# Output tiles by token parity, a last tile in two column halves and a shorter list of end waits, in a recurrent-attention and MLP kernel

## The chip, the cores and the metric

The kernel runs on one core of one Trainium2 chip. The metric is the device time of one execution in microseconds (us), smaller is better. A profiled execution also gives a span, from the first to the last instruction; it is about 1.7 us shorter than the device time of the same execution (182.9 against 184.67 us for the kernel before).

A result names a state for each run: slow when it is over 1.5% above the fastest run *of the same kernel in the same comparison*.

Names used below: TensorE is PE in the profile (its weight loads PEld), VectorE is DVE, ScalarE is ACT, GpSimd is POOL, SyncE is SP. Psum is the memory that the matmuls write here, a semaphore a counter that instructions wait for, and the granted clock the share of TensorE's full clock that the profile records.

## The reference

A gated recurrent attention feeds a two-layer MLP with a squared relu.

```python
# q, k, v, alpha: (4 batches, 8 heads, 768 tokens, 48), float32
state = zeros(B, H, D, D)
for t in range(S):
    state = alpha[:, :, t, :, None] * state + einsum('bhd,bhe->bhde', k[:, :, t], v[:, :, t])
    y[:, :, t] = einsum('bhd,bhde->bhe', q[:, :, t], state)
x = y.transpose(0, 2, 1, 3).reshape(3072, 384)
h = x @ w_in                       # 384 -> 2048
out = maximum(h, 0) ** 2 @ w_out   # 2048 -> 384, float32
```

## The kernel before

The work is cut into 12 units g of 256 tokens. A unit is loaded (alpha, k, q, v), its attention is computed in pairs of tokens, its output x is transposed into `XT`, and then the MLP runs: first layer (`s1`, weights w_in), relu, square, second layer (`s2`, weights w_out), store. A small list scheduler in the kernel orders every engine's instructions once, before the run, with modelled times; on the chip ACT, to take the engine that matters below, worked through its list in that order (in before_again it stood 8.07 us at one instruction, with the next in its list behind it).

A chunk of x holds 128 tokens in the partition order (parity j, pair t). The kernel before keeps that order through the first layer and lets the relu put the tokens back in sequence, by writing with a step of two elements:

```python
# s1: 6 matmuls of 256 columns into one 512-column psum half
rin  = psH[hb].rearrange("p (x j t) -> p x j t", j=2, t=64)
rout = RR[rb][:].rearrange("p (x t j) -> p x j t", j=2, t=64)      # step of 2 elements
add("act", lambda e: e.activation(rout, rin, AF.Relu), ..., alts={"dve": ...max(rin, 0)...})
# square into GT; s2: 16 matmuls of 384 columns per output tile of 128 consecutive tokens
r0 = b * S + i * T + 128 * jq
add("sp", lambda e: e.dma_start(out[r0:r0 + 128, :], OSB[ob][:]), ...)
```

The end waits for the semaphore of every DMA of the program:

```python
final = [(self.dma_sems[k], 16 * n) for k, n in self.dma_count.items()]    # 30 semaphores
...
if e == "sp":
    for s, v in final:
        eng.wait_ge(s, v)
```

The loads are gated on each other's landing (a number is a unit, `"a"` its alpha); the inputs go out from SP, the weights from GpSimd:

```python
AFTER = {("win", 0): (1, "a"), ("win", 1): (1, "a"), 2: ("win", 0), ("wout", 0): (2, "a"),
         ("wout", 1): (2, "a"), 3: ("wout", 0)}
```

Each unit's v is cast to bf16 on whichever of GpSimd and ACT the scheduler finds free first. For the third unit (g = 2) it chose ACT, in front of that unit's logarithm:

```python
add("pool", lambda e: e.tensor_copy(vout, vin), 830, p0 + 900, reads=[("raw", r, 3)], ...,
    name=f"vc{g}", alts={"act": (lambda e: e.activation(vout, vin, AF.Copy), act_ns(2 * HD))})
```

```text
ACT's list around it (from the built program):  ... relu, square,
  Activation vbf<-raw 128x768   waits for v of unit 2        <- the cast
  Activation lab<-prd           the ln of unit 2, needed by TensorE's next matmuls
```

## Time and profile before

| | us |
|---|---|
| timed runs | 194.54, 193.52, 195.4 (median 194.54) |
| the profiled run | 184.67 (span 182.9, granted clock 1.00) |

The page of the profile, engines (busy time, share of the span, instructions), and its chain of work that ended last, followed back from the last instruction, at each step to what released it:

```profile
PE 176.7 (97%) x2325; PEld 138.6 (76%) x2325; DVE 128.2 (70%) x220; ACT 127.6 (70%) x217; POOL 19.3 (11%) x27
...
PE 80%; DMA 15%; SPq 2%; issue 1%; ACT 0%
PE psO L828 34%; PE psWH L797 31%; DMA raw<-in_alpha_dram 6%; DMA win<-in_moe_w_in_dram 5%; DMA wout<-in_moe_w_out_dram 5%; PE psX L666 3%; PE psX L659 2%; PE psZ L639 2%; PE psX L720 2%; PE psX L759 2%; SPq L491 2%; PE psWH L537 2%; PE psX
```

TensorE is busy 97% of the span and holds 80% of the chain. Groups of instructions: line, engine, operation, output from input, count | busy us, mean ns | idle time before:

```profile
L807 ACT ACTIVATE rr<-psWH 128x512 bf16<-128x512 f32 x78 | 56.0, 754 | 16.4 <-PE psWH L797 16.4
...
L809 DVE TENSOR_SCALAR rr<-psWH 128x512 bf16<-128x512 f32 x18 | 13.2, 739 | 2.7 <-PE psWH L797 2.5
...
L747 ACT ACTIVATE xbf<-psX 128x768 bf16<-128x768 f32 x12 | 9.7, 810 | 9.4 <-PE psZ L639 7.0 <-PE psX L666 2.2
...
L551 ACT ACTIVATE eq<-psWH 128x384 f32<-128x384 f32 x10 | 4.9, 490 | 0.3
```

L807 is the relu with the step of two. L747 and L551 are other ACT instructions that read psum, 768 and 384 columns, without it, in 810 and 490 ns; between them 512 columns would take about 600 ns by my estimate, not 754.

The chain in order of time (start, us, what), until TensorE takes over:

```profile
4.30 4.88 DMA raw<-in_alpha_dram
9.47 8.55 DMA win<-in_moe_w_in_dram
18.04 5.69 DMA raw<-in_alpha_dram
24.02 8.38 DMA wout<-in_moe_w_out_dram
32.45 1.48 PE psO L828 x8
```

So there are three parts. The start is bound by loads: alpha of the second unit, w_in, alpha of the third, w_out. The middle starts with the first w_out matmul at 32.45 us and is bound by TensorE. The end begins at 174.6 us, with the last first-layer matmul. The table by stretches (length, then the busy us of PE, PEld, DVE, ACT and POOL, clock, DMA share, GB/s) cut at those two points:

```profile
0.00:32.40 32.40, 29.81 (x412) 23.90 (x412) 24.42 (x56) 22.04 (x35) 5.66 (x14) 1.00 1.01 232
32.40:174.60 142.20, 142.01 (x1884) 111.96 (x1885) 102.88 (x163) 103.47 (x179) 13.62 (x14) 1.00 0.73 168
174.60:182.90 8.30, 4.85 (x31) 2.77 (x29) 0.85 (x2) 2.06 (x4) 0.00 (x0) 1.00 0.13 47
```

TensorE is busy 142.01 of the 142.20 us in the middle. Nothing here explains why the timed runs are 10 us longer than the profiled one.

### The profile page before, as it was taken

What the parts mean: (1) busy time and instruction counts of PE and PEld (TensorE: products, weight loads), DVE (VectorE), ACT (ScalarE), POOL (GpSimd) and SP (SyncE); (2) the same over time, 40 slices, a digit from 0 to 9 for tenths busy, and PEclk for the clock granted to TensorE, in tenths of its full rate; (3) what the DMA queues carried; (4) which work ended last, traced back from release to release, by engine and by line L of the source; (5) the groups of instructions that cost most, each with busy time, mean ns of one, the idle gap of its engine ahead of it and who ended that gap; (6) DMA issues with size and microseconds to landing.
All of it is one profiled execution on the core that took longest, in us unless ns stands there. A gap on an engine that the chain in (4) does not pass through costs nothing.

```text
span 182.9 us, 5327 instructions
## 1 busy us (share of the span) xinstructions
PE 176.7 (97%) x2325; PEld 138.6 (76%) x2325; DVE 128.2 (70%) x220; ACT 127.6 (70%) x217; POOL 19.3 (11%) x27
## 2 busy tenths in 40 slices
PE   7998999999999999999999999999999999999992
PEld 5786886766788688787878787788787787788760
DVE  6399678797979988968978939769749736433220
ACT  4662899476878778679769868678667746677541
POOL 3030021123023011202103210000000000000000
PEclk9999999999999999999999999999999999999999
DMA  5999999999999999999999990713613410110202
GB/s 148 322 279 200 249 239 192 230 253 277 214 277 225 313 219 292 233 325 234 325 279 227 295 212 6 156 49 59 104 45 61 104 43 0 47 43 7 83 0 86
DMA packets 73495, 31.80 MB, mean 174 GB/s; under 512 B 69376, under 2 KB 72448, under 8 KB 73472
## 3 DMA queue, kind: packets, MB, share of 16 engines
q1 hardware_dynamic: 72384, 28.32, 65.3%
q0 software_dynamic: 1088, 3.15, 9.4%
q8 instruction: 18, 0.29, 0.6%
q14 instruction: 5, 0.04, 0.1%
HBM read 25.17 MB, written 4.72 MB: 163 GB/s over the span
## 4 chain that ended last, share of the span: by engine, by line
PE 80%; DMA 15%; SPq 2%; issue 1%; ACT 0%
PE psO L828 34%; PE psWH L797 31%; DMA raw<-in_alpha_dram 6%; DMA win<-in_moe_w_in_dram 5%; DMA wout<-in_moe_w_out_dram 5%; PE psX L666 3%; PE psX L659 2%; PE psZ L639 2%; PE psX L720 2%; PE psX L759 2%; SPq L491 2%; PE psWH L537 2%; PE psX L828 1%; PE psZ L720 1%; PE psZ L603 0%
## 5 line engine op out<-in xcount | busy, mean ns | idle before, releaser
L797 PE MATMUL psWH<-xt,win 128*128 128x256 bf16 x576 | 73.8, 275 | 0.6 <-DMA win<-in_moe_w_in_dram 0.5
L828 PE MATMUL psO<-wout,gt 128*128 128x384 bf16 x368 | 70.6, 327 | 0.6 <-DMA wout<-in_moe_w_out_dram 0.6
L797 PEld LDWEIGHTS psWH<-xt,win 128*128 128x128 bf16 x576 | 65.0, 145 | 5.7 <-DVE xt L765 0.9
L807 ACT ACTIVATE rr<-psWH 128x512 bf16<-128x512 f32 x78 | 56.0, 754 | 16.4 <-PE psWH L797 16.4
L828 PEld LDWEIGHTS psO<-wout,gt 128*128 128x128 bf16 x368 | 34.4, 98 | 19.2 <-DMA wout<-in_moe_w_out_dram 0.9
L813 DVE TENSOR_TENSOR gt<-rr 128x512 bf16<-128x512 bf16 x54 | 23.0, 431 | 21.8 <-ACT rr L807 21.5
L816 ACT ACTIVATE gt<-rr 128x512 bf16<-128x512 bf16 x41 | 25.2, 626 | 2.1 <-DVE rr L809 1.5
L835 ACT ACTIVATE osb<-psO 128x384 f32<-128x384 f32 x21 | 10.3, 491 | 12.7 <-PE psO L828 12.7
L747 ACT ACTIVATE xbf<-psX 128x768 bf16<-128x768 f32 x12 | 9.7, 810 | 9.4 <-PE psZ L639 7.0
L809 DVE TENSOR_SCALAR rr<-psWH 128x512 bf16<-128x512 f32 x18 | 13.2, 739 | 2.7 <-PE psWH L797 2.5
L729 DVE TENSOR_TENSOR pm<-psX,caus 128x1024 bf16<-128x1024 f32 x12 | 14.7, 1222 | 0.6 <-PE psZ L720 0.4
L729 DVE TENSOR_TENSOR pm<-psZ,caus 128x1024 bf16<-128x1024 f32 x12 | 14.6, 1217 | 0.1
L589 DVE TENSOR_TENSOR qks<-raw,ek 128x768 bf16<-128x768 f32 x12 | 11.7, 971 | 3.4 <-ACT ek L516 3.2
L878 PE MATMUL psO<-zero 128*128 128x256 bf16 x81 | 12.5, 309 | 1.3 <-DVE zero L412 1.3
L589 DVE TENSOR_TENSOR qks<-raw,eq 128x768 bf16<-128x768 f32 x12 | 11.4, 952 | 0.4 <-POOL eq L564 0.2
L692 DVE TENSOR_TENSOR tmp<-psZ,sbd 128x384 f32<-128x384 f32 x8 | 4.4, 555 | 9.2 <-PE psZ L639 9.2
L878 PEld LDWEIGHTS psO<-zero 128*128 128x128 bf16 x81 | 8.4, 110 | 3.0 <-DVE zero L412 1.2
L765 DVE COPY xt<-psX 128x768 bf16<-128x768 bf16 x10 | 5.6, 556 | 5.8 <-PE psX L759 5.8
L585 POOL CAST vbf<-raw 128x768 bf16<-128x768 f32 x6 | 5.7, 956 | 33.1 <-DMA raw<-in_v_dram 21.6
L666 PE MATMUL psX<-vbf,pm 64*128 64x48 bf16 x384 | 6.9, 181 | 0.0
L531 ACT ACTIVATE lab<-prd 128x384 bf16<-128x384 f32 x10 | 5.2, 516 | 1.9 <-DVE prd L528 1.5
L666 PEld LDWEIGHTS psX<-vbf,pm 64*128 64x128 bf16 x384 | 5.6, 93 | 0.8
(104 smaller groups left out, 159.4 us busy)
## 6 DMA issues: line engine op xcount, KB each, us to landing
raw<-in_alpha_dram SPq DMA_DIRECT2D x12, 384.0 KB, 4.5
raw<-in_k_dram SPq DMA_DIRECT2D x12, 384.0 KB, 4.8
raw<-in_q_dram SPq DMA_DIRECT2D x12, 384.0 KB, 5.2
raw<-in_v_dram SPq DMA_DIRECT2D x12, 384.0 KB, 5.2
out_dram<-osb SPq DMA_DIRECT2D x24, 192.0 KB, 2.6
win<-in_moe_w_in_dram POOLq DMA_DIRECT2D x2, 768.0 KB, 9.9
wout<-in_moe_w_out_dram POOLq DMA_DIRECT2D x2, 768.0 KB, 10.1
kqt<-qks SPq DMA_TRANSPOSE x18, 4.8
```

The lines of the kernel that those rows point to most:

```text
L589: add("dve", lambda e, a=a, E=E: e.tensor_tensor(QKS[qs][:, a, :, :, 0:D], RAW[r][:, 1 + a].rearrange("p h j d -> p j h d"), E[la][:].rear ...
L666: ins = pe.matmul(psX[:, c, h * D:(h + 1) * D], PM[pm][64 * c:64 * c + 64, n // 2, rr_, n % 2, jk, :], VBF[vb][64 * c:64 * c + 64, h, jk, ...
L729: add("dve", lambda e, hf=hf, psT=psT: e.tensor_tensor(PM[pm][:, hf].rearrange("p r n j t -> p (r n) (j t)"), psT[:, :, :].rearrange("p r ...
L747: add("act", lambda e: e.activation(XBF[x2][:], psX[:, :, 0:HD], AF.Copy), act_ns(2 * HD), p0 + 6100, reads=[("ps", "X", 0), ("ps", "X", 1 ...
L797: ins = pe.matmul(psH[hb][:, i * n:(i + 1) * n], WIN[:, kk, hidden(fj)], mov, start=(kk == 0), stop=(kk == KT - 1))
L807: add("act", lambda e, rin=rin, rout=rout: e.activation(rout, rin, AF.Relu), act_ns(512), pu + 600, reads=[("ps", "H", hb)], writes=[("rr" ...
L809: alts={"dve": (lambda e, rin=rin, rout=rout: e.tensor_scalar(rout, rin, 0.0, None, ALU.max), dve_ns(512))})
L813: add("dve", lambda e, dst=dst, sq=sq: e.tensor_tensor(dst, sq, sq, ALU.mult), 415, pu + 1200, reads=[("rr", rb)], writes=[("gt", gt, g0 + ...
L816: "act": (lambda e, dst=dst, sq=sq: e.activation(dst, sq, AF.Square), act_ns(512))})
L828: ins = pe.matmul(psS, GT[gt][:, fj, g0 + ui, jq, :], WOUT[:, fj, :], start=(fj == 0), stop=(fj == FT - 1))
L835: add("act", lambda e, ob=ob, psS=psS: e.activation(OSB[ob][:], psS, AF.Copy), act_ns(DM), ps_ + 700, reads=[keyS], writes=[("osb", ob)], ...
L878: pr.fill(lambda pe: pe.matmul(psO[:, 0:256], ZERO[:, 0:128], ZERO[:, 0:256], skip_group_check=True), 109, min(o.start for o in pr.order[" ...
```

## The change

The intent: take the strided write off the relu, by letting each output tile hold the tokens of one parity and storing it at a row stride of two; and shorten the end, with a last tile in two column halves, whose first store runs under the second half's matmuls, and with waits for the stores alone. The diff, cut to its core:

```diff
-        final = [(self.dma_sems[k], 16 * n) for k, n in self.dma_count.items()]
+        stores = {}
+        for o in sorted((o for o in self.ops if o.name.startswith("out")), key=lambda o: o.start):
+            stores.pop(o.sem[0], None)
+            stores[o.sem[0]] = o
+        final = [(self.dma_sems[k], self.value[o]) for k, o in stores.items()]     # 6 semaphores
 ...
+        to = bank[:, 0:KT * T].rearrange("p (k j c t) -> p c k j t", k=KT, j=2, c=2)
 ...                                              # transposes: token order (j, c, t) from here on
-                    ins = pe.matmul(bank[:, o * 128:(o + 1) * 128], src[:, ...], IDENT[:], is_transpose=True)
+                    ins = pe.matmul(to[:, c, kk], src[:, ...], IDENT[:], is_transpose=True)
 ...
-            rin = psH[hb].rearrange("p (x j t) -> p x j t", j=2, t=64)
-            rout = RR[rb][:].rearrange("p (x t j) -> p x j t", j=2, t=64)
-            add("act", lambda e: e.activation(rout, rin, AF.Relu), ...
+            add("act", lambda e: e.activation(RR[rb][:], psH[hb], AF.Relu), ...
 ...
-            r0 = b * S + i * T + 128 * jq
-            add("sp", lambda e: e.dma_start(out[r0:r0 + 128, :], OSB[ob][:]), ...
+            rows = slice(b * S + i * T + j, b * S + i * T + T, 2)
+            add("sp", lambda e: e.dma_start(out[rows, :], OSB[ob][:]), ...
 ...
+    def last_tile(gt, rows, p0):
+        n = DM // 2
+        for h in range(2):
+            psS, cut = psX[:, h, 0:n], slice(h * n, (h + 1) * n)
+            ...                                   # 16 matmuls of 192 columns
+            add("act", lambda e: e.activation(OSL[:, cut], psS, AF.Copy), ...
+            add("sp", lambda e: e.dma_start(out[rows, cut], OSL[:, cut]), ...
```

The lists of instructions of all engines, laid side by side, are the same before and after except in the last tile.

More of the change, by code (lines that the diff above doesn't have):

```diff
@@ L346, in bass_gla_recurrent__then__act_relu_squared_kernel @@
     units = [(b, i) for i in range(NST) for b in range(B)]
-    BLOCKS = [[g] for g in range(G)]
     PE_TRANSPOSED = 3
-    PE_X = G
     NRAW, NQKS, NKQT, NPM, NV, NXT, NGT, NRR, NOSB = 4, 3, 3, 2, 4, 4, 2, 4, 4
@@ L374, in bass_gla_recurrent__then__act_relu_squared_kernel @@
     XBF = sb("xbf", [128, 2, HD], BF16, 2)
-    XT = sb("xt", [128, 2, 2, KT, 128], BF16, NXT)
-    GT = sb("gt", [128, FT, 2, 2, 128], BF16, NGT)
+    XT = sb("xt", [128, KT, 2, 128], BF16, NXT)
+    GT = sb("gt", [128, FT, 2, 128], BF16, NGT)
     RR = sb("rr", [128, 512], BF16, NRR)
     OSB = sb("osb", [128, DM], FP32, NOSB)
+    OSL = nc.alloc_sbuf_tensor("osl", [128, DM], FP32)
     WIN = nc.alloc_sbuf_tensor("win", [128, KT, DFF], BF16)
@@ L480, in load @@
         first, last = i == 0, i == NST - 1
-        xt = XSLOT[g]
         sr, sw = 2 * b + i % 2, 2 * b + (i + 1) % 2
@@ L574, in front @@
         first, last = i == 0, i == NST - 1
-        xt = XSLOT[g]
         sr, sw = 2 * b + i % 2, 2 * b + (i + 1) % 2
@@ L749, in output, with xtr @@
             alts={"dve": (lambda e: e.tensor_copy(XBF[x2][:], psX[:, :, 0:HD]), dve_ns(2 * HD))})
-        s, slot = XSLOT[g]
+        s = g % NXT
         src = XBF[x2][:].rearrange("p c n -> p (c n)")
-        dst = XT[s][:, slot].rearrange("p c k t -> p (c k) t")
-        if g < PE_X:
-            bank = psX[:, 0, :].bitcast(BF16)
-            def xtr(pe):
-                for o in range(2 * KT):
-                    ins = pe.matmul(bank[:, o * 128:(o + 1) * 128], src[:, o * 128:(o + 1) * 128], IDENT[:],
-                                    is_transpose=True)
-                return ins
-            add("pe", xtr, pe_ns(6, 128), p0 + 6700, reads=[("xbf", x2), ("ident",)], writes=[("ps", "X", 0)],
-                name=f"xt{g}")
-            add("dve", lambda e: e.tensor_copy(dst.rearrange("p a t -> p (a t)"), bank[:, 0:768]), dve_ns(768, 2),
-                p0 + 7200, reads=[("ps", "X", 0)], writes=[("xt", s, slot)], name=f"xv{g}",
-                alts={"act": (lambda e: e.activation(dst.rearrange("p a t -> p (a t)"), bank[:, 0:768], AF.Copy),
-                              act_ns(768))})
-        else:
-            add(TR_RING, lambda e: e.dma_start_transpose(dst, src), 1300, p0 + 6700, reads=[("xbf", x2)],
-                writes=[("xt", s, slot)], name=f"xt{g}", dma=f"x{s}{slot}", lag=1400)
+        dst = XT[s][:].rearrange("p k j t -> p (k j t)")
+        bank = psX[:, 0, :].bitcast(BF16)
+        to = bank[:, 0:KT * T].rearrange("p (k j c t) -> p c k j t", k=KT, j=2, c=2)
+        def xtr(pe):
+            for c in range(2):
+                for kk in range(KT):
+                    o = c * KT + kk
+                    ins = pe.matmul(to[:, c, kk], src[:, o * 128:(o + 1) * 128], IDENT[:], is_transpose=True)
+            return ins
+        add("pe", xtr, pe_ns(6, 128), p0 + 6700, reads=[("xbf", x2), ("ident",)], writes=[("ps", "X", 0)],
+            name=f"xt{g}")
+        add("dve", lambda e: e.tensor_copy(dst, bank[:, 0:KT * T]), dve_ns(KT * T, 2),
+            p0 + 7200, reads=[("ps", "X", 0)], writes=[("xt", s)], name=f"xv{g}",
+            alts={"act": (lambda e: e.activation(dst, bank[:, 0:KT * T], AF.Copy), act_ns(KT * T))})
     rr_i = [0]
@@ L775, in bass_gla_recurrent__then__act_relu_squared_kernel, with s2, moe @@
     o_i = [0]
-    def moe(m, gs):
-        nu_ = len(gs)
-        n = nu_ * T
-        s = XSLOT[gs[0]][0]
-        per = 512 // n
-        p0 = gs[-1] * P + 20500
-        gt, g0 = GSLOT[m]
+    def last_tile(gt, rows, p0):
+        n = DM // 2
+        for h in range(2):
+            psS, keyS, cut = psX[:, h, 0:n], ("ps", "X", h), slice(h * n, (h + 1) * n)
+            def s2(pe, psS=psS, cut=cut):
+                for fj in range(FT):
+                    ins = pe.matmul(psS, GT[gt][:, fj, 1, :], WOUT[:, fj, cut], start=(fj == 0), stop=(fj == FT - 1))
+                return ins
+            add("pe", s2, pe_ns(FT, n), p0 + h, reads=[("gt", gt, fj) for fj in range(FT)]
+                + [("wout", w) for w in range(WS)], writes=[keyS], name=f"s2_{G - 1}_1_{h}")
+            add("act", lambda e, psS=psS, cut=cut: e.activation(OSL[:, cut], psS, AF.Copy), act_ns(n), p0 + 700 + h,
+                reads=[keyS], writes=[("osl", h)], name=f"oe{G - 1}_1{h}",
+                alts={"dve": (lambda e, psS=psS, cut=cut: e.tensor_copy(OSL[:, cut], psS), dve_ns(n))})
+            add("sp", lambda e, cut=cut: e.dma_start(out[rows, cut], OSL[:, cut]), 600, p0 + 1300 + h,
+                reads=[("osl", h)], name=f"out{G - 1}_1{h}", dma=f"l{h}", lag=400)
+    def moe(g):
+        b, i = units[g]
+        s, gt = g % NXT, g % NGT
+        per = 512 // T
+        p0 = g * P + 20500
         nb = FT // per
-        W = nu_ * P
         for u in range(nb):
@@ L789, in moe @@
             rr_i[0] += 1
-            pu = p0 + u * W * 0.5 / nb
+            pu = p0 + u * P * 0.5 / nb
             def s1(pe, u=u, hb=hb):
@@ L795, in s1 @@
                     for kk in range(KT):
-                        mov = XT[s][:, 0:nu_, :, kk, :].rearrange("p u c t -> p (u c) t")
-                        ins = pe.matmul(psH[hb][:, i * n:(i + 1) * n], WIN[:, kk, hidden(fj)], mov,
+                        ins = pe.matmul(psH[hb][:, i * T:(i + 1) * T], WIN[:, kk, hidden(fj)],
+                                        XT[s][:, kk].rearrange("p j t -> p (j t)"),
                                         start=(kk == 0), stop=(kk == KT - 1))
@@ L801, in moe @@
             fjs = range(u * per, (u + 1) * per)
-            add("pe", s1, pe_ns(KT * per, n), pu, reads=[("xt", s, i) for i in range(nu_)]
-                + sorted({("win", f // FS) for f in fjs}), writes=[("ps", "H", hb)], name=f"s1_{m}_{u}")
-            rin = psH[hb].rearrange("p (x j t) -> p x j t", j=2, t=64)
-            rout = RR[rb][:].rearrange("p (x t j) -> p x j t", j=2, t=64)
-            add("act", lambda e, rin=rin, rout=rout: e.activation(rout, rin, AF.Relu), act_ns(512), pu + 600,
-                reads=[("ps", "H", hb)], writes=[("rr", rb)], name=f"re{m}_{u}",
-                alts={"dve": (lambda e, rin=rin, rout=rout: e.tensor_scalar(rout, rin, 0.0, None, ALU.max),
+            add("pe", s1, pe_ns(KT * per, T), pu, reads=[("xt", s)] + sorted({("win", f // FS) for f in fjs}),
+                writes=[("ps", "H", hb)], name=f"s1_{g}_{u}")
@@ L810, in moe @@
+            add("act", lambda e, hb=hb, rb=rb: e.activation(RR[rb][:], psH[hb], AF.Relu), act_ns(512), pu + 600,
+                reads=[("ps", "H", hb)], writes=[("rr", rb)], name=f"re{g}_{u}",
+                alts={"dve": (lambda e, hb=hb, rb=rb: e.tensor_scalar(RR[rb][:], psH[hb], 0.0, None, ALU.max),
                               dve_ns(512))})
-            dst = GT[gt][:, u * per:(u + 1) * per, g0:g0 + nu_].rearrange("p f u c t -> p f (u c t)")
-            sq = RR[rb][:].rearrange("p (f t) -> p f t", f=per)
+            dst = GT[gt][:, u * per:(u + 1) * per].rearrange("p f j t -> p (f j t)")
@@ L813, in moe @@
+            sq = RR[rb][:]
             add("dve", lambda e, dst=dst, sq=sq: e.tensor_tensor(dst, sq, sq, ALU.mult), 415, pu + 1200,
-                reads=[("rr", rb)], writes=[("gt", gt, g0 + i, fj) for i in range(nu_) for fj in fjs], name=f"sq{m}_{u}",
+                reads=[("rr", rb)], writes=[("gt", gt, fj) for fj in fjs], name=f"sq{g}_{u}",
                 alts={"pool": (lambda e, dst=dst, sq=sq: e.tensor_tensor(dst, sq, sq, ALU.mult), 1040),
                       "act": (lambda e, dst=dst, sq=sq: e.activation(dst, sq, AF.Square), act_ns(512))})
-        for ti, (ui, jq) in enumerate((ui, jq) for ui in range(nu_) for jq in range(2)):
-            b, i = units[gs[ui]]
+        for j in range(2):
@@ L819, in moe, with s2 @@
             ob = o_i[0] % NOSB
             o_i[0] += 1
-            last = m == len(BLOCKS) - 1 and ti == 2 * nu_ - 1
-            psS, keyS = (psX[:, 0, 0:DM], ("ps", "X", 0)) if last else (psO[:, 0:DM], ("ps", "O"))
+            rows = slice(b * S + i * T + j, b * S + i * T + T, 2)
+            if g == G - 1 and j == 1:
+                last_tile(gt, rows, p0 + P)
+                continue
+            psS, keyS = psO[:, 0:DM], ("ps", "O")
             for sg in range(4):
-                ps_ = p0 + W * 0.5 + 600 + (ti * 4 + sg) * W * 0.5 / (8 * nu_)
-                def s2(pe, sg=sg, ui=ui, jq=jq, psS=psS):
+                ps_ = p0 + P * 0.5 + 600 + (j * 4 + sg) * P * 0.5 / 8
+                def s2(pe, sg=sg, j=j, psS=psS):
@@ L827, in s2 @@
                     for fj in range(sg * FT // 4, (sg + 1) * FT // 4):
-                        ins = pe.matmul(psS, GT[gt][:, fj, g0 + ui, jq, :], WOUT[:, fj, :],
+                        ins = pe.matmul(psS, GT[gt][:, fj, j, :], WOUT[:, fj, :],
                                         start=(fj == 0), stop=(fj == FT - 1))
@@ L832, in moe @@
                 add("pe", s2, pe_ns(FT // 4, DM), ps_,
-                    reads=[("gt", gt, g0 + ui, fj) for fj in range(sg * FT // 4, (sg + 1) * FT // 4)] + [("wout", sg * WS // 4)],
-                    writes=[keyS], name=f"s2_{m}_{ti}_{sg}")
+                    reads=[("gt", gt, fj) for fj in range(sg * FT // 4, (sg + 1) * FT // 4)] + [("wout", sg * WS // 4)],
+                    writes=[keyS], name=f"s2_{g}_{j}_{sg}")
             add("act", lambda e, ob=ob, psS=psS: e.activation(OSB[ob][:], psS, AF.Copy), act_ns(DM), ps_ + 700,
-                reads=[keyS], writes=[("osb", ob)], name=f"oe{m}_{ti}",
+                reads=[keyS], writes=[("osb", ob)], name=f"oe{g}_{j}",
                 alts={"dve": (lambda e, ob=ob, psS=psS: e.tensor_copy(OSB[ob][:], psS), dve_ns(DM))})
-            r0 = b * S + i * T + 128 * jq
-            add("sp", lambda e, ob=ob, r0=r0: e.dma_start(out[r0:r0 + 128, :], OSB[ob][:]), 600, ps_ + 1300,
-                reads=[("osb", ob)], name=f"out{m}_{ti}", dma=f"o{ob}", lag=600)
-    XSLOT = {g: (m % NXT, ui) for m, gs in enumerate(BLOCKS) for ui, g in enumerate(gs)}
-    GSLOT = {}
-    half = 0
-    for m, gs in enumerate(BLOCKS):
-        GSLOT[m] = (half // 2 % NGT, half % 2)
-        half += len(gs)
+            add("sp", lambda e, ob=ob, rows=rows: e.dma_start(out[rows, :], OSB[ob][:]), 600, ps_ + 1300,
+                reads=[("osb", ob)], name=f"out{g}_{j}", dma=f"o{ob}", lag=600)
     L_PRIO = {g: (g - 4) * P for g in range(G)}
@@ L875, in bass_gla_recurrent__then__act_relu_squared_kernel @@
             output(g, kind == "w")
-            moe(g, BLOCKS[g])
+            moe(g)
     pr.schedule()
```

## The prediction

> **What bounds the kernel now.** Up to 32.45 us it is the loads: the chain of waits runs alpha 4.9 us, w_in 8.6, alpha 5.7, w_out 8.4. From there to the last matmul it is TensorE: the table by stretches gives it 26.9 of 27 us in 33-60 and 30.0 of 30 in the next three stretches; the chain puts 80% of the span on TensorE, ACT under 1%. [...]256-column matmuls follow each other every 109 ns, 384-column ones every 163 ns, 2.35 columns per ns both, so TensorE really streams. After 33 us I find some 16 stalls between first-layer matmuls, about 55 ns each, 0.9 us together.
>
> **What the change does.**
> 1. Transposes now write tokens grouped by parity, so the relu no longer writes with a step of two elements. It takes 754 ns on ACT (x78); other ACT readers of PSUM take 487 ns for 384 and 810 for 768 columns, so a contiguous 512 should be about 600. Estimate: 78 x 0.15 = 12 us less ACT time, 1 us less on VectorE. [...]All of it is off the critical path and pays only through the stalls: two psum halves alternate, and a six-matmul group (0.655 us) outruns a 754 ns relu, not a 600 ns one. I credit 0.4 of the 0.9 us.
> 2. Every engine's instruction order is the same as before except at the end; no stage is rearranged. Transposes with outputs in two runs of 64 should keep their 56 ns spacing.
> 3. Stores with a row step of two still move 1536-byte rows: 2.6 us median to landing, unchanged, hidden.
> 4. Last tile in halves: 32 matmuls of 192 columns at about 82 ns = 2.64 us against 16 x 163 = 2.61: +0.03. Transposes show weights swapped every 56 ns, so weights don't bind. The last eviction falls from 491 to about 330 ns (-0.16); the last store carries half the bytes: its packets took 180.83 to 181.4 us, so -0.25.
> 5. End: after the last store's semaphore (181.87 us) SP still walks ten waits long satisfied, 61 ns each, before its branch at 182.54. One step at most remains after the last store: -0.55.
>
> **Sum.** 0.4 + 0.16 + 0.25 + 0.55 - 0.03 = 1.3 us, mostly tail: span 182.9 to about 181.6. The timed runs are 10 us longer than the profiled one for reasons that the profile doesn't show; I carry the same 1.3 us over: 194.5 to 193.2 us, range 191.7 to 194.7. Faster by over 2%: 0.04; within 2%: 0.95; slower: 0.01.
>
> **What would show each step.** ACT busy falls from 127.6 to about 116 us with relu near 600 ns, while TensorE stays above 96% busy and the chain keeps its 80%; first w_out matmul still at about 32.4 us; last matmul earlier by at most 0.5 us; from last matmul start to end of span about 2.5 us, not 3.5; one wait, not ten, after the last store landed.
>
> **What would make it wrong.** If relus held TensorE up in a way that the chain hides, the gain exceeds 2 us. If the timed runs' extra 10 us are ACT-bound or clocked differently, the relu might count more. If two-run PSUM writes slow the 72 transposes, or 192-column matmuls run slower than 82 ns (98 ns weight loads binding would add 0.5 us), the gain vanishes.

The sum came to 1.3 us.

## The result, and the profile after

| | runs, us | median |
|---|---|---|
| before | 194.54, 193.52, 195.4, 194.76 | 194.65 |
| after | 184.28, 181.91, 193.19, 182.15 | 183.22 |

The ratio was 0.9395 (95% interval 0.9294 to 0.9496), 6% faster, against 0.7% predicted; 183.22 us lies far below the stated range of 191.7 to 194.7. A ratio here is the mean time of one kernel's fast runs over that of the other's fast runs of the same rounds, so it is not quite the ratio of the medians. Of the changed kernel's four runs, 193.19 was slow, with a granted clock of 0.973. The four runs of before agree with each other.

The profiled runs, both at clock 1.00, give another picture: 184.67 us before, 184.28 after. The same lines of the profile after, page and chain first:

```profile
PE 176.8 (97%) x2341; PEld 139.8 (77%) x2341; DVE 128.2 (70%) x220; ACT 120.4 (66%) x218; POOL 18.7 (10%) x27
...
PE 70%; DMA 21%; DVE 3%; SPq 3%; issue 1%; ACT 1%
PE psO L842 30%; PE psWH L811 26%; DMA raw<-in_alpha_dram 9%; DMA wout<-in_moe_w_out_dram 5%; DMA win<-in_moe_w_in_dram 5%; DMA kqt<-qks 3%; PE psX L667 3%; PE psX L660 2%; SPq L493 2%; PE psX L721 2%; PE psZ L640 2%; PE psX L763 2%; PE psX
```

```profile
L819 ACT ACTIVATE rr<-psWH 128x512 bf16<-128x512 f32 x78 | 46.3, 596 | 19.4 <-PE psWH L811 17.8
...
L821 DVE TENSOR_SCALAR rr<-psWH 128x512 bf16<-128x512 f32 x18 | 12.3, 688 | 3.1 <-PE psWH L811 3.0
```

The relu takes 596 ns on ACT, as predicted (about 600), and 688 on VectorE, 0.9 us less busy in all (1 us was predicted), while TensorE is as busy as it was.

The chain in order of time, and the table by stretches, cut at the first w_out matmul (33.1 us) and the last first-layer matmul (175.1 us):

```profile
4.28 4.84 DMA raw<-in_alpha_dram
9.41 8.27 DMA win<-in_moe_w_in_dram
17.70 6.30 DMA raw<-in_alpha_dram
24.29 8.73 DMA wout<-in_moe_w_out_dram
33.08 1.47 PE psO L842 x8
```

```profile
0.00:33.00 33.00, 30.29 (x412) 24.02 (x412) 23.94 (x55) 20.86 (x35) 5.18 (x14) 1.00 0.99 228
33.00:175.10 142.10, 141.56 (x1884) 111.92 (x1885) 103.37 (x164) 97.43 (x180) 13.50 (x14) 1.00 0.74 168
175.10:182.50 7.40, 4.95 (x48) 3.82 (x45) 0.85 (x2) 2.06 (x5) 0.00 (x0) 1.00 0.16 53
```

ACT is busy 97.43 us in the middle instead of 103.47, and the middle is as long as before. The starts of single matmuls, read from the trace, cut the two spans more finely:

| part | before | after | difference |
|---|---|---|---|
| start, to the first w_out matmul | 32.45 | 33.08 | +0.62 |
| middle, to the last first-layer matmul | 142.18 | 142.08 | -0.09 |
| end | 8.31 | 7.37 | -0.93 |
| span | 182.94 | 182.53 | -0.41 |

The start runs the same loads in both kernels, so I take its +0.62 us for scatter of the loads, and the experiments below show scatter of that size and more. The end is 0.93 us shorter, the prediction's 0.55 + 0.25 + 0.16 - 0.03. The middle shows next to nothing of the 0.4 us that I credited to the shorter relu; one late load, after which TensorE starts nothing from 101.09 to 101.70 us, hides it in this profile (more below). So the profiled pair agrees with the prediction about the end, and the timed runs do not agree with it at all. Where do the timed runs' 10 us come from?

### The profile page after: what moved, and what is told of

Same layout as the page of the kernel before. It is cut to its first block, busy times and chain, and to the rows that moved or that the text cites. A ratio compares the mean times of both kernels' runs of the same rounds, so it can differ in the third digit from the quotient of the medians.

```text
span 182.5 us, 5348 instructions
## 1 busy us (share of the span) xinstructions
PE 176.8 (97%) x2341; PEld 139.8 (77%) x2341; DVE 128.2 (70%) x220; ACT 120.4 (66%) x218; POOL 18.7 (10%) x27
## 3 DMA queue, kind: packets, MB, share of 16 engines
q0 software_dynamic: 1088, 3.15, 9.4%
## 4 chain that ended last, share of the span: by engine, by line
PE 70%; DMA 21%; DVE 3%; SPq 3%; issue 1%; ACT 1%
PE psO L842 30%; PE psWH L811 26%; DMA raw<-in_alpha_dram 9%; DMA wout<-in_moe_w_out_dram 5%; DMA win<-in_moe_w_in_dram 5%; DMA kqt<-qks 3%; PE psX L667 3%; PE psX L660 2%; SPq L493 2%; PE psX L721 2%; PE psZ L640 2%; PE psX L763 2%; PE psX L784 1%; PE psWH L539 1%; PE psZ L721 1%
## 5 line engine op out<-in xcount | busy, mean ns | idle before, releaser
L819 ACT ACTIVATE rr<-psWH 128x512 bf16<-128x512 f32 x78 | 46.3, 596 | 19.4 <-PE psWH L811 17.8
L825 DVE TENSOR_TENSOR gt<-rr 128x512 bf16<-128x512 bf16 x54 | 23.6, 445 | 18.6 <-ACT rr L819 17.9
L821 DVE TENSOR_SCALAR rr<-psWH 128x512 bf16<-128x512 f32 x18 | 12.3, 688 | 3.1 <-PE psWH L811 3.0
L587 ACT ACTIVATE vbf<-raw 128x768 bf16<-128x768 f32 x6 | 5.0, 841 | 3.2 <-DMA raw<-in_v_dram 3.2
L564 DVE TENSOR_TENSOR ek<-ek,raw 128x384 f32<-128x384 f32 x10 | 6.2, 619 | 0.9 <-ACT ek L551 0.9
```

Source lines behind the costliest of these rows:

```text
L819: add("act", lambda e, hb=hb, rb=rb: e.activation(RR[rb][:], psH[hb], AF.Relu), act_ns(512), pu + 600, reads=[("ps", "H", hb)], writes=[(" ...
L821: alts={"dve": (lambda e, hb=hb, rb=rb: e.tensor_scalar(RR[rb][:], psH[hb], 0.0, None, ALU.max), dve_ns(512))})
L825: add("dve", lambda e, dst=dst, sq=sq: e.tensor_tensor(dst, sq, sq, ALU.mult), 415, pu + 1200, reads=[("rr", rb)], writes=[("gt", gt, fj) ...
```

## The experiments

Sixteen kernels ran, in four groups; the kernels of one group ran on the same chip with their own runs of the kernel before, in rounds. All results were correct. The run that is listed first is the profiled one.

### First group: is it the kernel at all?

Theory A: the 6% is a lower granted clock that fell on the runs of before, from outside. Theory B: the old kernel brings it about itself, with its strided relu.

**before_again** is the kernel before, unchanged, against itself.

> The kernel before, unchanged, timed against itself. Theory A (clock state): the 5.9% of the first result is a lower granted TensorE clock that fell on the before runs, whatever the kernel; then runs of this program come in two groups, about 184 us at clock 1.00 and about 194 us at about 0.97, and it is within 0.5% of itself where both are fast. Theory B (the old kernel itself brings the slow time about): nearly all runs of it are near 194 us again while those of the changed kernel are near 182.

Measured: all six of its runs were slow, 193.18 to 195.44 us, median 193.62, while the same program under the name of before ran 184.79, 193.22, 184.01, 185.57, 194.31, 195.87, 193.49, 193.87, 184.62, 184.8, 185.0 in the same rounds. The ratio of a kernel to itself came out at 1.0493 (interval 1.0433 to 1.0553). There are two groups of times, near 185 and near 194 us, for one program; the first result had compared one group with the other.

**after_again** is the changed kernel, unchanged.

> The changed kernel again. Theory A: runs at clock 1.00 take 181.9 to 182.5 us, 0.7 to 1.2% under before at clock 1.00 on the same chip; slow runs about 193 us, again about 1% under slow runs of before. Theory B: 5 to 6% faster than before, with before at 194.

Measured: 192.06, 183.48, 182.06, 191.69, 191.36, 184.91. It has both groups too. Its fast runs give 0.989 of the fast runs of before (0.9812 to 0.9969). The rule told 184.91 slow as well, 1.6% above 182.06, though its clock was 1.00; with it the means give 0.993.

**layout_only** is the changed kernel with the parity layout and the row-step stores kept and the rest undone:

```diff
-        final = [(self.dma_sems[k], self.value[o]) for k, o in stores.items()]
+        final = [(self.dma_sems[k], 16 * n) for k, n in self.dma_count.items()]
-            if g == G - 1 and j == 1:
-                last_tile(gt, rows, p0 + P)
-                continue
 ...                                               # the last tile is written whole, as before
```

> The parity layout and the row-step stores alone; last tile whole, all 30 end waits. Theory A: 0.2 to 0.6 us under before in the same state (relu 596 ns, a third of the first-layer stalls gone), tail as before. Theory B: 5% faster than before, since it is the strided relu that costs the 10 us.

Measured: 193.75, 183.02, 184.75, 183.66, 193.26, 189.6; ratio 0.9946 (0.988 to 1.0013). With the relu at its short time the slow runs still come, so the relu as the cause (theory B) is out. The run of 189.6 (clock 0.989) lies between the groups, has no trace and stays unexplained.

**tail_only** is the kernel before with the other half of the change:

```diff
-        final = [(self.dma_sems[k], 16 * n) for k, n in self.dma_count.items()]
 ...
+        final = [(self.dma_sems[k], self.value[o]) for k, o in stores.items()]
 ...
+            if last:
 ...
+                last_tile(gt, g0 + ui, jq, slice(r0, r0 + 128), p0 + W)
+                continue
```

> The old layout with the last tile in two column halves and the short list of end waits. Theory A: 0.9 to 1.1 us under before in the same state, nothing else different. Theory B with the relu as cause: slow like before, about 193 us.

Measured: 184.49, 184.56, 182.78, 183.48, 192.35, 184.45; ratio 0.9954 (0.99 to 1.0008).

Theory A in the form "from outside" did not survive the profiles, though. Three profiled runs of this group fell among the slow ones. The page of before_again (span 191.8 us, slices of 4.8 us; the rows are the busy share of TensorE, its granted clock, and the DMA engines' busy share, in tenths):

```profile
PE   7998990399999999999999999999999999999992
...
PEclk9999998559999999999999999999999999999999
DMA  5999999920699999999999996241721701110102
```

The clock is low in only two or three slices, and TensorE is idle *before* it: 0 in the seventh slice, 28.8 to 33.6 us. ACT's instructions there (start, us, what, idle before it and what ended it):

```profile
26.63 0.61 ACT L816 ACTIVATE gt<-rr 128x512 bf16<-128x512 bf16 x1
35.32 0.84 ACT L586 ACTIVATE vbf<-raw 128x768 bf16<-128x768 f32 x1 [8.07 <-DMA raw<-in_v_dram]
36.07 0.51 ACT L531 ACTIVATE lab<-prd 128x384 bf16<-128x384 f32 x1
```

ACT stands 8.07 us at the cast of v until v has landed, and the ln of the third unit, which follows it in ACT's list, waits with it. In the fast profile the same lines are:

```profile
26.52 0.61 ACT L816 ACTIVATE gt<-rr 128x512 bf16<-128x512 bf16 x1
27.24 0.84 ACT L586 ACTIVATE vbf<-raw 128x768 bf16<-128x768 f32 x1
28.00 0.51 ACT L531 ACTIVATE lab<-prd 128x384 bf16<-128x384 f32 x1
```

The chain of before_again says the same:

```profile
22.48 12.82 DMA raw<-in_v_dram
...
35.32 0.84 ACT vbf L586
36.16 0.42 ACT lab L531
...
36.63 0.50 PE psWH L537
```

Why does one v take 12.8 us? Landing times and packets, read from the trace's DMA records:

```text
                         v of unit 2      first half of w_out   v's 384 B packets    w_out's 6144 B packets
                         issued  landed   issued  landed        at 27.5 to 33.5 us   at 27.5 to 33.5 us (mean)
before (fast)            21.85   27.22    24.02   32.41          0                   194 (504 ns)
before_again (slow)      22.48   35.30    23.91   31.20         55                   205 (479 ns)
```

Theory R, then: a race of loads. w_out goes out on the software queue (`q0 software_dynamic` on the page, 1088 packets) when alpha of the third unit has landed, while v of that unit is still on its way on the hardware queue (`q1 hardware_dynamic`, 72384). Where v's last packets get through first, nothing happens (in before none of them fell in the 6 us of the table). Where some DMA engines still hold v packets when the large w_out packets start (in before_again ten of the sixteen had delivered their part of v by 27.2 us, the other six between 27.9 and 35.3), the small packets, by this theory, wait for large ones, v lands some 8 us late (35.30 us against 27.22), ACT stops at the cast (8.07 us), TensorE starves (8.01 us before its next matmul at 36.63), and then runs at half clock for a while.

### Second group: move the cast, move the loads

**before_cast_pool** moves that one instruction, after the scheduling, from ACT's list to GpSimd's, behind a multiplication of the same unit; nothing else changes place:

```diff
     pr.schedule()
+    op = {o.name: o for o in pr.ops}
+    cast, at = op["vc2"], op["aq2"]
+    pr.order["act"].remove(cast)
+    cast.eng, (cast.fn, cast.cost) = "pool", cast.alts["pool"]
+    pr.order["pool"].insert(pr.order["pool"].index(at) + 1, cast)
     ...                                                # renumber the lists (asserts and modelled times left out)
```

> Before, with one instruction moved: the cast of v of the third unit from ACT (where it stands in front of the third unit's ln) to GpSimd, behind work that is done by then. Theory R (race of loads): the slow runs come from v of the third unit landing at 35 us instead of 27, because its 384-byte packets meet the 6144-byte packets of w_out; ACT waits for it in order, TensorE starves 8 us and then runs 10 us at half clock. Then without the cast in ACT's way v may still land late, but no run is above 187 us; median 183.5 to 185. Theory A (a clock state of the chip from outside): slow runs of 193 us as often as before.

Measured: 183.94, 184.56, 185.89, 184.12, 184.32, 183.78; no slow run. Before beside it: 4 slow of 11 (193.19 to 193.72), the rest 184.28 to 184.98. Ratio 0.9991 to the fast runs of before.

**after_cast_pool**: the same diff on the changed kernel.

> The changed kernel with the same one instruction moved. Theory R: all runs 182 to 183.5 us, none slow, and 1.0 to 1.6 us (0.5 to 0.9%) under the old kernel with the cast moved: the change's own gain without the race. Theory A: slow runs of 191 us appear.

Measured: 185.06, 183.36, 183.73, 183.29, 183.3, 184.53; no slow run. The profiled one of these (185.06) had lost the race: v landed at 37.35 us by the trace. All the same ACT went on and the clock stayed at 1.00:

```profile
27.75 0.62 ACT L828 ACTIVATE gt<-rr 128x512 bf16<-128x512 bf16 x1
28.64 0.52 ACT L533 ACTIVATE lab<-prd 128x384 bf16<-128x384 f32 x1 [0.28 <-DVE prd L530]
```

```profile
PEclk9999999999999999999999999999999999999999
```

The gain over before_cast_pool is 0.68 us by the medians (183.54 against 184.22), less than I had written, and the runs of each scatter by about 2 us.

**before_v_late** should have lost the race every time, by one more wait on v's load, which goes out when alpha of the same unit has landed (modelled times left out here and in the next diffs):

```diff
+    op["ldv2"].deps[op["lda2"]] = True
```

> Before, with the load of v of the third unit issued 1.5 to 2 us later (it waits for alpha to land, as w_out does), so that it always meets w_out. Theory R: every run slow, 192 to 197 us, clock 0.97 to 0.98. Theory A: fast runs of 184 to 186 us about as often as before.

Measured: 183.54, 184.29, 192.85, 193.25. This was a miss: two runs were fast. In the profiled one, a fast run, v was issued at 23.69 us instead of 21.85, but landed at 27.15, no later than before (27.22): issuing it 1.8 us later did not move it. My estimate, from the landings alone (k, q and v at 24.71, 25.90 and 27.15 us): its packets stood behind those of k and q anyway. The two slow runs have no trace.

**before_wout_late** lets w_out wait for v instead of alpha:

```diff
+    for w in ("wout0", "wout1"):
+        del op[w].deps[op["lda2"]]
+        op[w].deps[op["ldv2"]] = True
```

> Before, with w_out issued only when v of the third unit has landed (about 2.5 us later). Theory R: no run near 193; every run 186 to 188.5 us, since w_out itself then comes 2 to 3 us late and TensorE waits for it. Theory A: slow runs as often as before, near 195.

Measured: 188.56, 185.83, 186.06, 186.61; no slow run, but 1.2% above the fast runs of before (ratio 1.0117). Keeping w_out away from v is free of slow runs near 193 us in these four, and costs its own delay. The profiled run, the slowest, shows the cast's cost in small too: v landed at 28.51 us, ACT stood 2.00 us at the cast, and the clock was at half for one stretch of 3.41 us.

### Third group: force the race, with and without the cast in ACT's way

**layout_cast_pool** and **tail_cast_pool** are layout_only and tail_only with the diff of before_cast_pool.

> Parity layout and row-step stores alone, with the v cast moved so that no slow runs come. Theory (the change is worth its small sum): relu near 596 ns and ACT 7 us less busy, but time within 0.4 us of the old kernel with the cast moved (184.2 us); the end unchanged, ten waits after the last store. Rival (relus hold TensorE up more than the chain shows): over 1 us faster.

Measured: 184.66, 183.37, 185.26, 183.93, 187.7, 184.32, median 184.49; ratio 0.9955 (0.9899 to 1.0012). No run near 193, but one of 187.7 whose cause I have not looked into; no gain clear of the scatter.

> Old layout, last tile in two halves and the short list of waits, with the v cast moved. Theory: from the start of the last tile's part to the end of the span 0.9 to 1.1 us shorter; time about 183.3 us, no slow run. Rival: no gain in time, since the start's scatter or a later wait takes it back.

Measured: 183.75, 183.42, 182.98, 184.0, 184.24, 184.29; ratio 0.9927 (0.988 to 0.9973). In its trace the end, from the last first-layer matmul, is 7.52 us, against 8.30 in layout_cast_pool and 8.31 in before: the end's gain belongs to the last tile and the waits. That run had also lost the race (v landed at 34.86 us) and took 183.75 us, as after_cast_pool's had.

**before_v_later** puts v behind the landing of q, at about 25.6 us, so that w_out is certainly under way:

```diff
+    op["ldv2"].deps[op["ldq2"]] = True
```

> Before, with v of the third unit loaded only after q has landed, at about 26 us, when w_out is already on its way: the race is always lost. Theory R: every run slow, 192 to 196 us, TensorE idle about 8 us from 28 us on, then half clock for some 7 to 10 us. Theory A: fast runs at 184 to 186 us appear.

Measured: 193.85, 194.05, 194.16, 194.5. Every run is slow, at a clock of 0.973 in the profiled one. ACT again:

```profile
35.64 0.84 ACT L586 ACTIVATE vbf<-raw 128x768 bf16<-128x768 f32 x1 [8.37 <-DMA raw<-in_v_dram]
36.39 0.51 ACT L531 ACTIVATE lab<-prd 128x384 bf16<-128x384 f32 x1
```

**before_v_later_cast_pool** has this diff and that of before_cast_pool together: the same late v, and the cast moved.

> The same late load of v, but the cast moved to GpSimd. Theory R: v lands at 35 to 37 us in every run, yet every run is 183.5 to 186 us and the clock stays at 1.00, since only the place of the cast in ACT's order makes the late v costly. Theory A or a rival in which late v itself holds TensorE: slow runs, 190 us or more.

Measured: 183.9, 184.2, 184.58, 184.43. v lands at 35.69 us here, within the range of the five slow profiles (34.90 to 36.12), and every run is fast. First the lines of ACT here that answer to the last fence; then the table of busy time from 28 to 37 us (columns as before), for before_v_later and after it for this kernel:

```profile
27.33 0.52 ACT L531 ACTIVATE lab<-prd 128x384 bf16<-128x384 f32 x1 [0.18 <-DVE prd L528]
...
28.84 0.49 ACT L549 ACTIVATE ek<-psWH 128x384 f32<-128x384 f32 x1 [0.46 <-PE psWH L541]
```

```profile
28.00:37.00 9.00, 0.69 (x7) 0.41 (x6) 1.94 (x4) 1.36 (x3) 0.00 (x0) 0.73 1.05 248
```

```profile
28.00:37.00 9.00, 8.92 (x111) 7.26 (x110) 8.45 (x14) 6.70 (x13) 2.48 (x3) 1.00 1.07 250
```

TensorE is busy 0.69 of those 9 us with the cast on ACT and 8.92 with it on GpSimd. So it takes both: the late v, and the cast in front of the ln in ACT's list. Over all groups 46 runs had the cast on GpSimd, and the longest of them took 187.7 us.

The packets tell how v is held up. With v forced late (before_v_later), from 29 to 33 us, per microsecond and over all 16 DMA engines: 15, 35, 34 and 43 packets of 384 bytes, beside 33, 32, 32 and 32 of 6144. Once w_out is through, 822 small packets of all loads pass between 34 and 35 us. So in these four microseconds the two kinds passed nearly one for one, 127 small against 129 large, at some 475 ns for each large packet.

### Fourth group: the change's own gain, on a steady start

The late v with the moved cast had given the narrowest scatter (0.7 us), so I compared the kernels on that start.

**base_both** is before_v_later_cast_pool once more.

> The old kernel with the late load of v and the moved cast once more, as the base of the next two: 183.9 to 184.6 us again, no slow run.

Measured: 185.1, 184.62, 184.52, 184.54, 184.18, 184.49, median 184.53.

**after_v_later_cast_pool** is the changed kernel with the same two diffs.

> The changed kernel on the same start. If the change is worth its tail only: 0.9 us under that base, 183.3 us. If the shorter relu also wins back stalls of TensorE as predicted: 1.3 us under it. No slow run.

Measured: 182.68, 183.07, 183.01, 182.88, 183.03, 182.79, median 182.95. The means are 184.58 and 182.91 us: 1.67 us less, a ratio of 0.991 to base_both. To the fast runs of before it is 0.9919 (0.9899 to 0.9938), and no run was slow. This is the best version found. It beats the changed kernel too, whose ten runs average 186.7 us because four of them lost the race; the fastest of those, 181.91 us, is faster than any run here.

**layout_v_later_cast_pool** is layout_only with the two diffs.

> Layout and row-step stores alone on the same start. Tail-only theory: within 0.2 us of the base. Stall theory: 0.4 us under it.

Measured: 184.98, 184.13, 184.1, 183.23, 184.02, 184.55, mean 184.17: 0.41 us under base_both. That is what the stall theory had asked for, but the runs of the two kernels overlap and their intervals against before (0.9945 to 1.0011, and 0.9985 to 1.0033) do too. It leans to the stall theory and doesn't settle it; the traces do, below.

**after_v_later** is the changed kernel with the diff of before_v_later, so with the late v and the cast left on ACT.

> The changed kernel with the late load of v and the cast left on ACT. If the change does nothing against the race: every run slow, about 193.2 us, 0.9 us under the old kernel in that state (194.1), clock 0.97. If it protects from it: runs near 183 us.

Measured: 193.08, 192.53, 192.66, 192.93. All slow, at a clock of 0.973 in the profiled run. The change does nothing against the race; it is worth about 1.3 us in the slow group too (mean 192.80 against 194.14 for before_v_later, on another chip).

The runs of 189.38 (before, in the fourth group) and 187.7 us have no trace and stay unexplained.

## Why the prediction was right or wrong

**Where it failed.** The step is this one: "The timed runs are 10 us longer than the profiled one for reasons that the profile doesn't show; I carry the same 1.3 us over". It took the 10 us for an offset that both kernels share. They are one of two outcomes of a race in the load phase, which the old kernel, by its times, lost in all four runs that the result used (none has a trace) and won in the profiled one. Over the four groups the runs named before (without the six of before_again) had 26 at 183.7 to 185.9 us, 18 at 193.0 to 195.9, and one at 189.4; the changed kernel, in all its runs, 6 at 181.9 to 184.9 and 4 at 191.4 to 193.2. The 6% is the distance between the two groups of times, not the worth of the change; that the old kernel drew the slow outcome four times of four and the changed one once of four is luck, as far as the runs show. An unexplained 10 us in the baseline also called for a much wider range.

**What the slow outcome costs.** In before_again TensorE starts no matmul for 8.3 us after 28.35 us, and the recorded clock is at half from 32.0 to 42.2 us. Matmuls of 256 columns start every 213 ns until then, and every 109 ns after. The first w_out matmul comes at 41.68 us instead of 32.45: 9.2 us later. The middle and the end are 141.81 and 8.31 us, as in the fast run. The clock fell 3.6 us after the last matmul had started; in the other four slow profiles it was 3.0 to 5.6 us. The stretch at half clock, between two at full, lasted 10.24 us in four of the five slow profiles, 6.83 in layout_only and 3.41 in before_wout_late; from the first matmul after the idle stretch to full clock it took 3.9 us in layout_only, 5.6 in before_again and 6.0 in after_again.

**The relu, right in size.** 754 to 596 ns on ACT, 739 to 688 on VectorE. (The step of two came with an access pattern of more dimensions; no run separates the two.) The durations of ACT's 78 relus add up to 46.5 us instead of 58.8, the 12 us predicted. ACT's busy time fell by 7.2 us only, not the 11.6 that I gave, because neighbouring instructions overlap: the durations of all ACT instructions add up to 11.9 us less, but two relus in a row, for one, had taken 1.40 us together, less than twice 754 ns.

**Its worth, about 0.3 us.** I credited 0.4 us of 0.9 us of stalls. The fast pair of profiles shows 0.09 us in the middle, and the fourth group 0.41 us between means, with overlapping runs. All 18 traces together settle it. From the start of the fifth unit's x transposes to the last first-layer matmul, TensorE takes 104.18 to 104.30 us in the ten with the old relu, and 103.93 in six of the eight with the short one; the other two, after and layout_only, take 104.34 and 104.37, each with one gap of 0.6 us. After 45 us the stalls between first-layer matmuls (starts over 125 ns apart, the excess over 109) are 15 to 17 with the old relu, 0.79 to 0.89 us, and 10 or 11 with the short one, 0.53 to 0.61. So the mechanism held, and 0.4 was somewhat too much.

**The end, right.** From the last first-layer matmul to the end of the span 0.93 us less, as summed. The parts, by the trace: last eviction 491 to 331 ns; last store from issue to semaphore 1.87 to 1.64 us; from that semaphore's wait to the end of the span 1.06 to 0.46 us, with ten waits fewer behind it; before's SP had taken these, long satisfied, one every 61 ns. The narrow matmuls start every 83 ns, where 82 was forecast, so the weight loads, 98 ns each in the trace, don't hold them up.

**Nothing rearranged, right.** Transposes keep their 56 ns; TensorE stays 97% busy. The chain's share of TensorE fell to 70%, not 80% as I had said: the loads took over the difference, in a start that scatters and in one late load and transpose near 92 to 102 us.

**The change's own worth.** 1.67 us, 0.9%, on the steady start, where I had said 1.3 us. The traces place 0.93 us of it in the end and about 0.3 in the stalls, 1.2 together; the rest may be the start, whose length still differs between the profiles there (31.46 to 32.52 us). In the other groups it is 1.1% in the first (by two runs that counted as fast; 0.7% with the third at clock 1.00) and 0.3% between the means of the two kernels with the cast moved, with more scatter.

**What stays open.** Why one build of the kernel lost the race six times of six while the identical program beside it lost five of eleven, and so why the first comparison fell out so one-sided. The runs show the two outcomes and what each costs, not what tips them. The traces do hold an earlier sign of it, which no run tested: how long SP takes to issue q of the third unit, just before v. Before first, then before_again:

```profile
19.08 2.73 SPq L491 DMA_DIRECT2D raw<-in_q_dram  x1
21.85 1.80 SPq L491 DMA_DIRECT2D raw<-in_v_dram  x1
```

```profile
19.20 3.23 SPq L491 DMA_DIRECT2D raw<-in_q_dram  x1
22.48 1.12 SPq L491 DMA_DIRECT2D raw<-in_v_dram  x1
```

In the ten profiles whose loads are gated as in before, that issue took 2.73 to 2.82 us in the five where v landed by 28.4 us, and 3.23 to 4.13 us in the five where it landed at 34.8 us or later. So the race looks decided before w_out goes out, at 23.4 us or later; why the issue takes longer is not shown.

## What to carry to other kernels

When the timed runs and the profiled run of one kernel differ by several per cent, there is a mechanism to find before any change is costed: time the kernel against itself, and look for the stretch that is idle in the slow profile and not in the fast one. A low mean clock can be the trace of an idle stretch and not its cause (0.973 in before_again, where the clock fell 3.6 us after the last matmul had started). In an engine's list, don't put an instruction that waits for a load, and whose result is needed late, in front of one that the bottleneck needs now (in before_v_later ACT stood 8.37 us at it, and the runs took 9.9 us more than with the cast moved), least of all where another queue's large packets can delay that load (in before_again v landed at 35.30 us instead of 27.22, beside w_out's packets of 6144 bytes).
